# Attention and a squared-ReLU layer on one core: a third set of q and k turned by the DMA crossbar, and a new order of loads

## The chip, the core and the metric

The kernel runs on one core of one Trainium2 chip. The time is the device time of one execution in microseconds (us). The profile comes from one further execution; its span, from the first to the last instruction, is about 2 us shorter than the device time of the same run (212.7 against 214.51).

## What is computed

Four batches, eight heads, 768 positions and 64 elements a head. Each position attends to the 96 positions up to and including its own and to the first 8 positions; a bias falls linearly with the distance, by a slope of each head. The result goes through a layer of 512 to 2048 with a squared ReLU and back to 512.

```python
scores = (q @ k.T) / sqrt(64) - slope[h] * dist      # kept: local (96) or global (first 8)
a = softmax(scores)                                  # per head
x = (a @ v)                                          # heads side by side: 3072 x 512
h = maximum(x @ w_in, 0)                             # 512 x 2048
out = (h * h) @ w_out                                # 2048 x 512
```

Inputs and output are float32; the kernel works in float16 with float32 sums.

## The kernel before

The 3072 rows are cut into eight **half batches** of 384 rows, numbered 0 to 7; batch b holds the halves 2b and 2b+1, and a half is three tiles of 128 rows. While TensorE computes the two layers of one half, the attention of the next half is laid between its matmuls. Halves 0 and 1 are the opening, and are worked through tile by tile.

A list scheduler in the kernel (`Plan`) lays out all operations by estimated durations and writes them in that order, engine by engine. The PE queue and the queue of loads keep the order in which they are listed; all else is placed by its estimated readiness. So constants such as a load's duration or an operation's `lag` change the order in which instructions stand, not what they do.

All loads are cast from float32 to float16 and issued by GpSimd (POOL). Half 0 and 1 and half 2 are turned (q and k brought to the layout with the head's elements on partitions) by TensorE transposes into PSUM, with copies by ACT or DVE behind them. Halves 3 to 7 are turned by the DMA crossbar, issued by SyncE (SP), as are the stores of the output and the turning of the attention's result into the layer's input `xt`:

```python
def list_loads(x):
    prev = halves[x.hb - 2] if x.hb >= 2 else None
    before = (prev.turned if prev else []) + ([*halves[x.hb - 1].turned, prev.x_ops[NPAIR - 1]] if x.hb > 3 else [])
    ...
            if x.hb > 3 and name == "sq" and t == 0:
                for turn in halves[x.hb - 1].turns + halves[x.hb - 2].turns[-1:]:
                    behind(dma, turn)                  # this load waits for those crossbar transfers
    ...
        x.q_in = [rows(q, "sq", t) for t in range(HT)]      # three loads of 128 rows each
        x.k_in = [rows(k, "sk", t) for t in range(HT)]
        x.v_in = [rows(v, "v", t) for t in range(HT)]

def turn(x, a):                                        # half 2 alone, pair of heads a
    # six 128x128 transposes into one PSUM bank, two copies to qk
    ...
                    nc.tensor.transpose(out=trp[:, i, t, :], in_=st[:, t, 2 * a:2 * a + 2, :],
                                        identity=ident)

def turn_by_dma(x):                                    # halves 3 to 7
    for i, (name, loads) in enumerate((("sk", x.k_in), ("sq", x.q_in))):
        def emit(e, i=i, name=name):
            turn = nc.sync.dma_start_transpose(
                out=x.bt.qk[:, 1 - i, ts]..., in_=getattr(x, name)...)
            if not x.turns:
                behind(turn, x.last_load)              # the first waits for the last load of q and k
            x.turns.append(turn)
        op = plan.add({"SP": 1.7}, emit, [*loads, x.bt.op, *late])
        op.lag = 2.5
    for a in range(NPAIR):
        x.qk_ops[a] = x.turned + [plan.add(*fix_k(x, a), x.turned[:1], wait=4.0)]   # kb: small DVE copies

def to_x_by_dma(x, a):                                 # xt, one crossbar transfer for each of 4 pairs
    ...
            x.turns.append(nc.sync.dma_start_transpose(out=x.xt[:, a, :]..., in_=st["tm"]...))
```

`score` issues the q-k products (`sp`, line 464), `attend` the products with v (`av`, line 519), `layer1` the first layer (`hps`, line 560; it needs `xt` of all four pairs), `layer2` the second (`yps`, line 609; four steps of four matmuls for each tile of 128 rows). `PLACES` says after how many steps of the layers each score, turn and attend of the next half stands; `OPENING` is the order on TensorE of the first two halves (T turns a tile, S scores it, A attends, X turns the result, F, G, D, E are parts of layer 1), and `LOADING` the order of the first loads (v, k and q by tile, c the quarters of `w_in`). `warm` adds matmuls on zeros where the plan sees a gap in the opening.

```python
for name in OPENING.split():
    jobs[name]()
for job in l1(x1, 8) + l2(x0)[:6]:
    job()
for hb in range(1, NHB):
    x = halves[hb]
    for y in halves[2:4] if hb == 1 else halves[hb + 2:hb + 3]:
        list_loads(y)
    main = l2(x0)[6:] + l2(x) if hb == 1 else l1(x) + l2(x)
    side = attention(halves[hb + 1]) if hb + 1 < NHB else []
    merge(main, side)
    if hb + 2 < NHB:
        turn_by_dma(halves[hb + 2])
```

Of the kernel before, what the change touches and what calls it, by code (L numbers as in the profile page):

```python
# [16 lines left out]

OPENING = """T0 T2 S0o S1b A01 S1o A00 T3 S2b X01 S2o A10 A11 T4 S3b V1 X00 X11 A21 S4o A20 F1 X21 S3o  # L20
X10 S4b X20 F0 G00 V2 T5 V3 V4 G11 A30 G10 A31 S5o G30 G31 S5b A41 G01 F3 X30 G21 A40 X31 F2
X40 X41 G20 A50 E00 A51 E01 E11 X50 X51 E10 D0 D1"""

LOADING = """v0 k2 q2 k3 v2 v1 q3 v4 k4 q4 c1 c0 q5 k5 v3 c3 v5 c2"""

PLACES = {2: (3, 7, 7, 9, 10, 11, 1, 0, 1, 0),
          0: (0, 9, 7, 11, 16, 18), 1: (0, 9, 9, 11, 17, 19)}


class Op:
# [113 lines left out]
def kernel(  # L149
# [42 lines left out]
    def bank(shape, dtype, name, i=0):  # L192
        return ps_p.tile(shape, dtype, name=name, tag=f"ps{plan.now[i]}")
# [4 lines left out]
    def copy(e, out, in_):  # L198
        if e == "ACT":
            nc.scalar.copy(out=out, in_=in_)  # L200
        else:
            eng(e).tensor_copy(out=out, in_=in_)  # L202
# [5 lines left out]
    def warm(ps):  # L208
        fp32 = ps.dtype == FP32
        n = min(512, ps.shape[-1]) if fp32 else P  # L210
        for _ in range(int(plan.spare / (n / 2400 + 0.003))):
            if fp32:
                nc.tensor.matmul(ps[:, 0:n], lhsT=zero[:, 0:P], rhs=zero[:, 0:n], start=True,
                                 stop=True)
            else:
                nc.tensor.transpose(out=ps[:, 0:n], in_=zero[:, 0:P], identity=ident)
# [85 lines left out]
    def list_loads(x):  # L302
        r0 = x.half * HALF
        prev = halves[x.hb - 2] if x.hb >= 2 else None
        before = (prev.turned if prev else []) + ([*halves[x.hb - 1].turned, prev.x_ops[NPAIR - 1]] if x.hb > 3 else [])
        vbefore = [halves[x.hb - x.half - 3].attended[-1]] if x.hb >= 4 else []

        def rows(src, name, t, rank=None):
            def emit(e):
                dst = (x.bt.v[:, x.half * HT + t, :, 0:D] if name == "v"  # L310
                       else staged(x, name)[:, t, :, :])
                dma = nc.gpsimd.dma_start(out=dst, in_=src[x.b, :, r0 + t * P:r0 + (t + 1) * P, :]  # L312
                                          .rearrange("h p d -> p h d"))
                if x.hb > 3 and name == "sq" and t == 0:
                    for turn in halves[x.hb - 1].turns + halves[x.hb - 2].turns[-1:]:
                        behind(dma, turn)
                if name == "sk":
                    x.last_load = dma
            return plan.load(0.86, emit, vbefore if name == "v" else before, rank,
                             1.6 if x.hb == 0 else 2.6)  # L320

        if x.half == 0:
            def start(e):
                new_batch(x.bt)
                nc.vector.memset(x.bt.v[:, :, :, D:D + 1], 1.0)
            x.bt.op = plan.add({"DVE": 0.1}, start, vbefore, rank=0)
        if x.hb > 1:
            x.q_in = [rows(q, "sq", t) for t in range(HT)]
            x.k_in = [rows(k, "sk", t) for t in range(HT)]
            x.v_in = [rows(v, "v", t) for t in range(HT)]  # L330
        else:
            x.k_in, x.q_in, x.v_in = [None] * HT, [None] * HT, [None] * HT
            for t in range(HT):
                r = x.half * HT + t
                if r > 1:
                    for src, name, key, ops in ((k, "sk", "k", x.k_in), (q, "sq", "q", x.q_in)):
                        load_jobs[f"{key}{r}"] = lambda src=src, name=name, ops=ops, t=t: (
                            ops.__setitem__(t, rows(src, name, t, -3 if not plan.queues["LOAD"]
                                                    else None)))
                load_jobs[f"v{r}"] = lambda t=t: (  # L340
                    x.v_in.__setitem__(t, rows(v, "v", t)), x.v_in[t].needs.append(x.bt.op))
            return
        for l in x.v_in:
            l.needs.append(x.bt.op)
        x.bt.v_in = [*getattr(x.bt, "v_in", []), *x.v_in]
# [24 lines left out]
            out=w_in_sb[:, :, c * n:(c + 1) * n],  # L370
            in_=moe_w_in[:, c * n:(c + 1) * n].rearrange("(k p) f -> p k f", p=P)))

    def list_w_out():
        n = NFT // 4
        for c in range(4):
            w_out_op.append(plan.load(2.55, lambda e, c=c: nc.gpsimd.dma_start(
                out=w_out_sb[:, c * n:(c + 1) * n, :],
                in_=moe_w_out[c * n * P:(c + 1) * n * P, :].rearrange("(m p) d -> p m d", p=P))))

# [13 lines left out]
    def fix_k(x, a):  # L393
        t0, t1 = tiles_before(x)

        def emit(e):
            kt = x.bt.qk[:, 1, :, a, :]
            copy(e, x.bt.kb[:, a, t0 - 1:t1 - 1, GR:P], kt[:, t0:t1, GR:P])
            copy(e, x.bt.kb[:, a, t0 - 1:t1 - 1, 0:GR],
                 kt[:, 0:1, 0:GR].to_broadcast([P, t1 - t0, GR]))  # L400
        return {"DVE": 0.2 + 0.08 * (t1 - t0)}, emit

    def turn(x, a):
        state = {}

        def emit(e):
            state["ps"] = trp = bank([P, 2, HT, P], FP16, "trp")
            warm(trp.rearrange("p i t c -> p (i t c)"))
            for i, st in enumerate((x.sq, x.sk)):
                for t in range(HT):  # L410
                    nc.tensor.transpose(out=trp[:, i, t, :], in_=st[:, t, 2 * a:2 * a + 2, :],  # L411
                                        identity=ident)
        job = plan.pe(6 * 0.056, emit, x.q_in + x.k_in + [ident_op], 1)

        def evac(i):
            def emit(e):
                copy(e, x.bt.qk[:, i, x.half * HT:(x.half + 1) * HT, a, :], state["ps"][:, i])
            return plan.after(job, {"ACT": 0.39, "DVE": 0.31}, emit)
        ops = [evac(0), evac(1)]
        x.turned.append(job)  # L420
        x.qk_ops[a] = ops + [plan.add(*fix_k(x, a), [ops[1]])]


    def turn_by_dma(x):
        ts = slice(x.half * HT, (x.half + 1) * HT)
        late = list(halves[x.hb - 2].x_ops.values()) if x.hb > 3 else []
# [3 lines that stand above are left out]
                    out=x.bt.qk[:, 1 - i, ts].rearrange("p t a c -> p (t a) c"),  # L430
                    in_=getattr(x, name).rearrange("p t h d -> p (t h d)"))
                if not x.turns:
                    behind(turn, x.last_load)
                x.turns.append(turn)
            op = plan.add({"SP": 1.7}, emit, [*loads, x.bt.op, *late])
            op.lag = 2.5
            x.turned.append(op)
        for a in range(NPAIR):
            x.qk_ops[a] = x.turned + [plan.add(*fix_k(x, a), x.turned[:1], wait=4.0)]
# [356 lines left out]
    def attention(x):  # L796
        jobs = []
        places = PLACES[x.hb if x.hb == 2 else x.half]
        for k in range(len(TOGETHER[x.half])):
            jobs.append((places[k], lambda k=k: score(x, k)))  # L800
        for a in range(NPAIR):
            if x.hb == 2:
                jobs.append((places[6 + a], lambda a=a: turn(x, a)))
            jobs.append((places[2 + a], lambda a=a: attend(x, a)))
            jobs.append((places[2 + a], lambda a=a: to_x_by_dma(x, a)))
        return sorted(jobs, key=lambda j: j[0])
# [28 lines left out]
    for name in LOADING.split():  # L835
# [6 lines left out]
                           rank=0) for h in range(H)]  # L842
    mask_ops = [plan.add({"ACT": 0.43}, lambda e, h=h: fill_mask(h), [dist_op], rank=10 + h)
                for h in range(H)]
    list_w_out()

    jobs = {}
    for r in range(NT):
# [17 lines left out]
        job()  # L866
    for hb in range(1, NHB):
        x = halves[hb]
        for y in halves[2:4] if hb == 1 else halves[hb + 2:hb + 3]:
            list_loads(y)  # L870
        if hb == 1:
            fix_v(halves[2].bt, 1, 2)
        main = l2(x0)[6:] + l2(x) if hb == 1 else l1(x) + l2(x)
        if hb == NHB - 1:
            main = main[:-NFT // 4] + [lambda: last_layer2(x, HT - 1)]
# [3 lines that stand above are left out]
            t0, t1 = tiles_before(halves[hb + 2])  # L879
            for t in range(t0, t1):  # L880
                fix_v(halves[hb + 2].bt, t, t + 1)
            turn_by_dma(halves[hb + 2])
# [37 lines left out]
```

The softmax here doesn't subtract the row's maximum and nothing guards it: scores larger than these inputs give would overflow.

## Time and profile before

| | |
|---|---|
| device time, median of 3 runs | 214.99 us (214.2 to 215.36) |
| span of the profiled run | 212.7 us, granted TensorE clock 1.000 |
| TensorE busy (PE) | 206.0 us, 97% |
| VectorE (DVE), ScalarE (ACT), GpSimd (POOL) busy | 116.7, 122.0, 66.6 us |
| DMA of the loads (q0), of SP's transfers (q1) | 13.11 MB each |
| layer 2 starts on TensorE (first `yps`) | 45.04 us |
| layer 1 of half 2 starts (`hps` after the first scores of half 3) | 70.63 us |

In the profile every instruction has its engine, its line of the kernel, and its tiles as "out<-in". PEld is TensorE's loading of weights, which runs beside its matmuls. SPq and POOLq are the sequencers that issue DMAs; for such a row the duration is that of issuing, and "to landing" is the time from the start of issue until the data are there. Line numbers are those of the kernel before.

### The profile page before, as it was taken

Reading aid. Unit: us, or ns where it says so; the run is one execution under the profiler, and the core shown is the slowest. Engines: PE = TensorE matmul, PEld = TensorE weight load, DVE = VectorE, ACT = ScalarE, POOL = GpSimd, SP = SyncE. Lnnn points to the kernel's source line nnn. Section 1 sums busy time; section 2 is a strip of 40 time slices with the busy share of each in tenths; the row PEclk is TensorE's granted clock in tenths of the full one; section 3 lists DMA queues with packets and bytes.
Section 4 is the critical chain, followed back from the end, with each engine's and each line's share of the span. In section 5 each row is a group of like instructions: output and inputs, shape, how many; then the busy total and the mean of one; then the engine's idle time right before and its main releaser. Section 6 shows DMA issues by size and latency. Waiting matters only on the chain.

```text
span 212.7 us, 4804 instructions
## 1 busy us (share of the span) xinstructions
PE 206.0 (97%) x1908; PEld 127.3 (60%) x1908; DVE 116.7 (55%) x334; ACT 122.0 (57%) x250; POOL 66.6 (31%) x82
## 2 busy tenths in 40 slices
PE   6799999999999999999999999999999999999994
PEld 7587889755464565456654665456644665456553
DVE  7598987443582579409770679219860777114300
ACT  6789985644741885148821994148811994237421
POOL 8994643694000940095006800094000000000000
PEclk9999999999999999999999999999999999999999
DMA  6999999999935999599976997299952100320012
GB/s 176 166 174 188 191 207 210 161 154 163 201 120 154 107 154 154 133 118 172 148 113 119 158 135 146 73 137 177 130 121 99 52 18 19 89 99 2 0 52 99
DMA packets 106343, 27.06 MB, mean 127 GB/s; under 512 B 96976, under 2 KB 103376, under 8 KB 106320
## 3 DMA queue, kind: packets, MB, share of 16 engines
q0 software_dynamic: 74944, 13.11, 80.2%
q1 hardware_dynamic: 30320, 13.11, 26.7%
q10 hardware_dynamic: 1056, 0.52, 0.8%
q8 instruction: 15, 0.25, 0.5%
q14 instruction: 8, 0.07, 0.1%
HBM read 27.26 MB, written 6.29 MB: 158 GB/s over the span
## 4 chain that ended last, share of the span: by engine, by line
PE 93%; DMA 3%; POOL 1%; DVE 1%; ACT 0%; issue 0%; POOLq 0%
PE hps L560 40%; PE yps L609 37%; PE sp L464 4%; PE av L519 4%; DMA sq<-in_q_dram 3%; PE yps L637 2%; PE sp L721 2%; PE av L760 1%; PE sp L714 1%; PE trp L669 1%; PE trx L787 1%; PE trp L411 1%; POOL v L312 0%; POOL sk L312 0%; DVE tm L772 0%; ACT qk L200 0%
## 5 line engine op out<-in xcount | busy, mean ns | idle before, releaser
L560 PE MATMUL hps<-xt,w_in_sb 128*128 128x384 f16 (+2 forms) x608 | 88.5, 301 | 0.0
L609 PE MATMUL yps<-w_out_sb,h 128*128 128x512 f16 x368 | 83.0, 379 | 0.0
L560 PEld LDWEIGHTS <-w_in_sb 128*128 128x128 f16 x608 | 53.8, 98 | 26.6
L584 ACT ACTIVATE hr<-hps 128x384 f16<-128x384 f32 (+1 forms) x106 | 54.9, 526 | 14.4 <-PE hps L560 13.3
L609 PEld LDWEIGHTS <-h 128*128 128x128 f16 x368 | 34.9, 98 | 39.0
L200 ACT COPY y<-yps 128x512 f32<-128x512 f32 (+1 forms) x25 | 14.2, 569 | 66.4 <-PE yps L609 63.8
L595 DVE TENSOR_TENSOR h<-hr 128x768 f16<-128x768 f16 (+1 forms) x70 | 35.5, 519 | 23.2 <-ACT hr L584 22.8
L312 POOL DMA_DIRECT2D sq<-in_q_dram x22 | 19.4, 889 | 66.0 <-DMA xt<-tm 64.3
L477 ACT ACTIVATE ex<-sp 128x512 f16<-128x512 f32 x66 | 35.0, 621 | 1.2 <-PE sp L464 1.2
L586 DVE TENSOR_SCALAR hr<-hps 128x384 f16<-128x384 f32 (+1 forms) x16 | 9.0, 562 | 39.4 <-PE hps L560 39.4
L312 POOL DMA_DIRECT2D v<-in_v_dram x24 | 21.7, 926 | 4.4 <-DMA w_out_sb<-in_moe_w_out_dram 3.7
L497 DVE TENSOR_TENSOR phat<-ex,mask 128x1024 f16<-128x1024 f16 (+1 forms) x36 | 20.2, 596 | 2.4 <-ACT ex L477 2.4
L312 POOL DMA_DIRECT2D sk<-in_k_dram x22 | 19.5, 901 | 5.0 <-DMA w_out_sb<-in_moe_w_out_dram 3.1
L529 DVE TENSOR_TENSOR tm<-av,rec 128x384 f16<-128x384 f32 x24 | 13.4, 557 | 0.8
L519 PEld LDWEIGHTS <-phat 128*128 128x128 f16 x240 | 9.8, 97 | 3.1
L519 PE MATMUL av<-v,phat 128*128 128x65 f16 x144 | 10.9, 193 | 0.0
L202 DVE COPY vb<-v 128x520 f16<-128x520 f16 (+1 forms) x32 | 9.9, 309 | 1.6 <-DMA v<-in_v_dram 0.9
L519 PE MATMUL av<-vb,phat 128*128 128x65 f16 x96 | 10.1, 194 | 0.0
L202 DVE COPY kb<-qk 128x96 f16<-128x96 f16 (+4 forms) x56 | 8.1, 203 | 2.0 <-ACT qk L200 2.0
L464 PEld LDWEIGHTS <-qk 64*128 64x128 f16 x168 | 6.3, 94 | 4.6 <-issue 3.7
L464 PE MATMUL sp<-qk 64*128 64x128 f16 x168 | 8.8, 218 | 0.0
L527 DVE RECIPROCAL rec<-av 128x6 f32<-128x6 f32 x24 | 4.7, 194 | 7.0 <-PE av L519 6.6
(66 smaller groups left out, 136.6 us busy)
## 6 DMA issues: line engine op xcount, KB each, us to landing
out_dram<-y SPq DMA_DIRECT2D x23, 256.0 KB, 2.2
v<-in_v_dram POOLq DMA_DIRECT2D x24, 128.0 KB, 6.5
sk<-in_k_dram POOLq DMA_DIRECT2D x22, 128.0 KB, 6.2
sq<-in_q_dram POOLq DMA_DIRECT2D x22, 128.0 KB, 5.6
w_in_sb<-in_moe_w_in_dram POOLq DMA_DIRECT2D x4, 512.0 KB, 10.1
w_out_sb<-in_moe_w_out_dram POOLq DMA_DIRECT2D x4, 512.0 KB, 14.1
y<-in_k_dram ACTq DMA_DIRECT2D x2, 256.0 KB, 4.9
y<-in_q_dram SPq DMA_DIRECT2D x2, 256.0 KB, 4.4
```

The costliest lines, as they stand in the source:

```text
L200: nc.scalar.copy(out=out, in_=in_)
L202: eng(e).tensor_copy(out=out, in_=in_)
L312: dma = nc.gpsimd.dma_start(out=dst, in_=src[x.b, :, r0 + t * P:r0 + (t + 1) * P, :] .rearrange("h p d -> p h d"))
L464: nc.tensor.matmul(sp[h][:, i, :], lhsT=lhsT, rhs=bt.qk[rows, 0, r, a, :], start=True, stop=True)
L477: nc.scalar.activation(out=st["ex"][:, h], in_=sp[h], func=AF.Exp, scale=scale)
L497: eng(e).tensor_tensor(out=x.phat[a][:, :, t0:t0 + n], op=ALU.mult, in0=st["ex"][:, :, i0:i0 + 2 * n].rearrange("p e (t b) c -> p e t (b c ...
L519: nc.tensor.matmul(av[:, h, j, :], lhsT=lhsT, rhs=rhs, start=not before, stop=before or r == 0)
L529: nc.vector.tensor_tensor(out=st["tm"].rearrange("p t e d -> p e t d"), in0=av[:, :, :, 0:D], in1=rec[:, :, :, None].to_broadcast([P, 2, H ...
L560: nc.tensor.matmul(st["ps"][:, i * n:(i + 1) * n], lhsT=w_in_sb[:, kk, m * P:(m + 1) * P], rhs=x.xt[:, kk, c0:c1], start=kk == 0, stop=kk ...
L584: nc.scalar.activation(out=o, in_=i, func=AF.Relu)
L595: eng(e).tensor_tensor(out=x.h2[:, m0:m0 + width, c0:c1], in0=hr, in1=hr, op=ALU.mult)
L609: nc.tensor.matmul(st["ps"], lhsT=x.h2[:, m, j * P:(j + 1) * P], rhs=w_out_sb[:, m, :], start=m == 0, stop=m == NFT - 1)
```

## The change

Half 2 is now turned by the crossbar like halves 3 to 7, so that its TensorE transposes and their PSUM copies fall away (`turn` is gone). For that its q and k must be there earlier: their six loads are listed ahead of the last quarter of `w_out`. The loads of half 3 now wait until half 2's crossbar transfers have landed, as the loads of the later halves already did for their predecessors. Order of the opening and of the first loads, and the places of half 2's scores and attends and of the odd halves' attends, are new.

```diff
-OPENING = """T0 T2 S0o S1b A01 S1o A00 T3 S2b X01 S2o A10 A11 T4 S3b V1 X00 X11 A21 S4o A20 F1 X21 S3o
-X10 S4b X20 F0 G00 V2 T5 V3 V4 G11 A30 G10 A31 S5o G30 G31 S5b A41 G01 F3 X30 G21 A40 X31 F2
-X40 X41 G20 A50 E00 A51 E01 E11 X50 X51 E10 D0 D1"""
+OPENING = """T0 T2 S0o S1o S2b V1 S1b A00 T3 V2 A01 S2o A10 S3o A11 A21 T4 X11 X01 S3b A20 X00 T5 X21 S4o
+X20 X10 F1 S4b A31 G11 V3 G10 G01 F0 A41 X31 A30 G00 S5b A40 F3 X30 G30 F2 X41 V4 X40 S5o
+G21 E10 E00 E11 A50 G20 A51 X50 G31 X51 E01 D0 D1"""
-LOADING = """v0 k2 q2 k3 v2 v1 q3 v4 k4 q4 c1 c0 q5 k5 v3 c3 v5 c2"""
+LOADING = """v1 q2 k2 k3 q3 v0 v2 q5 q4 k4 k5 c1 v3 c0 v4 c3 c2 v5"""
-PLACES = {2: (3, 7, 7, 9, 10, 11, 1, 0, 1, 0),
-          0: (0, 9, 7, 11, 16, 18), 1: (0, 9, 9, 11, 17, 19)}
+PLACES = {2: (5, 7, 8, 10, 11, 12),
+          0: (0, 9, 7, 11, 16, 18), 1: (0, 9, 9, 12, 17, 18)}
...
-        before = (prev.turned if prev else []) + ([*halves[x.hb - 1].turned, prev.x_ops[NPAIR - 1]] if x.hb > 3 else [])
+        before = (prev.turned if prev else []) + (halves[x.hb - 1].turned if x.hb > 2 else [])
+        before = before + ([prev.x_ops[NPAIR - 1]] if x.hb > 3 else [])
...
-                if x.hb > 3 and name == "sq" and t == 0:
+                if x.hb > 2 and name == "sq" and t == 0:
...
+            if x.hb == 2:
+                list_w_out(0, 3)
             x.q_in = [rows(q, "sq", t) for t in range(HT)]
             x.k_in = [rows(k, "sk", t) for t in range(HT)]
+            if x.hb == 2:
+                list_w_out(3, 4)
             x.v_in = [rows(v, "v", t) for t in range(HT)]
...
-            w_out_op.append(plan.load(2.55, ...
+            w_out_op.append(plan.load(2.55 if c < 3 else 3.6, ...
...
-    def turn(x, a):                       # the whole function falls away
...
-            op.lag = 2.5
+            op.lag = 2.5 if x.hb > 2 else 5.5
...
-            if x.hb == 2:
-                jobs.append((places[6 + a], lambda a=a: turn(x, a)))
...
-    list_w_out()
+    list_loads(halves[2])
+    turn_by_dma(halves[2])
...
-        for y in halves[2:4] if hb == 1 else halves[hb + 2:hb + 3]:
+        for y in halves[3:4] if hb == 1 else halves[hb + 2:hb + 3]:
```

In the built programs TensorE has 30 matmuls fewer: the 24 transposes of half 2, and six of the matmuls on zeros in the opening. SP issues two crossbar transfers more, ahead of all stores of the output; half 3's two crossbar transfers stand ahead of half 2's four `xt` transfers on SP, as before.

More of the change, by code (lines that the diff above doesn't have):

```diff
@@ L371, in load_w_in, with list_w_out @@
             in_=moe_w_in[:, c * n:(c + 1) * n].rearrange("(k p) f -> p k f", p=P)))
-    def list_w_out():
+    def list_w_out(c0, c1):
         n = NFT // 4
-        for c in range(4):
-            w_out_op.append(plan.load(2.55, lambda e, c=c: nc.gpsimd.dma_start(
+        for c in range(c0, c1):
+            w_out_op.append(plan.load(2.55 if c < 3 else 3.6, lambda e, c=c: nc.gpsimd.dma_start(
                 out=w_out_sb[:, c * n:(c + 1) * n, :],
@@ L401, in fix_k @@
         return {"DVE": 0.2 + 0.08 * (t1 - t0)}, emit
-    def turn(x, a):
[L404 to L421, printed above, removed]
     def turn_by_dma(x):
```

## The prediction

> **What bounds the kernel now.** I read the busy shares first, then the waits of TensorE alone, then its chain in order of time around half 2, then SP's own timeline, because the change moves work from TensorE to SP and the DMA engines.
>
> ```profile
> PE 206.0 (97%) x1908; PEld 127.3 (60%) x1908; DVE 116.7 (55%) x334; ACT 122.0 (57%) x250; POOL 66.6 (31%) x82
> ```
>
> TensorE is busy 97% of the span; no other engine passes 57%. The waits of PE from 9.5 us to the end are these two rows (us in total, times, longest):
>
> ```profile
> PE trp L669 <- DMA sq<-in_q_dram: 1.0, 1, 1.0
> PE sp L721 <- ACT qk L200: 0.4, 1, 0.4
> ```
>
> The first ends at 9.49 us. After it TensorE waits 0.4 us once, at 18.4 us. So what is taken off TensorE comes off the time, unless a new wait arises. The chain of work, in order of time (start, us, what), around half 2:
>
> ```profile
> 45.04 5.18 PE yps L609 x24
> 50.22 0.67 PE trp L411 x12
> ...
> 51.75 0.67 PE trp L411 x12
> ...
> 69.86 0.78 PE sp L464 x24
> ```
>
> These show the removed work (L411: 12 transposes in 0.67 us, twice) and the stage's end: layer 1 of half 2 starts at 70.63. SP in the same stage:
>
> ```profile
> 53.35 1.54 SPq L429 DMA_TRANSPOSE qk<-sq  x1
> 54.99 2.16 SPq L429 DMA_TRANSPOSE qk<-sk  x1
> 57.20 1.40 SPq L624 DMA_DIRECT2D out_dram<-y  x2
> 60.34 1.19 SPq L541 DMA_TRANSPOSE xt<-tm  x1
> 62.99 0.33 SPq L624 DMA_DIRECT2D out_dram<-y  x1
> 63.42 3.85 SPq L541 DMA_TRANSPOSE xt<-tm  x3
> ```
>
> The first two rows turn half 3. SP issues in order, so half 2's four xt transfers stand behind them. The last xt lands at 68.38 by the trace, 2.25 us before 70.63 needs it. That reserve, not the 57% of any engine, is what the change may use up.
>
> **What the Trainium skill says.** "VectorE: DVE Perf Modes", section "The three transpose paths", gives one 128x128 turn 390 ns on TensorE and 1309 ns by crossbar. The trace has 56 ns each in a row of 12 on TensorE (0.67/12), and 4.4 us from issue to landing for the 12 blocks of half 3's q. Both see the crossbar as the slower path; it pays only where its time is hidden. "DMA: Bandwidth & Descriptors", section "Issuing engines are not separate DMA queues", says that transfers from all issuers interleave on the same 16 DMA engines. The trace agrees: a 256 KB store issued by SP at 49.14, while POOL's loads filled the engines, needed 5.9 us to land, against a median of 2.2:
>
> ```profile
> out_dram<-y SPq DMA_DIRECT2D x1, 256.0 KB, 5.9
> out_dram<-y SPq DMA_DIRECT2D x23, 256.0 KB, 2.2
> ```
>
> (the first from the DMA issues of 42 to 56 us, the second from the page). No page bears on the order of the opening.
>
> **The change part by part.**
>
> 1. *Transposes removed.* 2 x 0.67 = 1.34 us off TensorE, all on the path. Their eight PSUM copies (five on ACT at 488 ns, three on DVE) lay beside it and bring nothing.
>
> 2. *The opening.* From 9.49 to 45.04 TensorE has 35.55 us. In it lie 0.44 us of idle time and seven matmuls on zeros: three of 0.056 us (0.17) and four that take 0.46 (11.70 to 12.16). The most that an order can bring is so 1.07 us. The new order keeps one such matmul. By the order of the two built programs it puts 22 more real matmuls ahead of F1 (about 22 x 0.056 = 1.22 us), so F1 would start at 9.49 + (9.68 - 1.07) + 1.22 + 0.11 = 19.43. Its quarter c1 of w_in is now the 12th load: the tenth landed at 15.87, one more is about 0.95 and a quarter 2.45, so 19.3: in time. c0 comes at 19.3 + 1.0 + 2.5 = 22.8, while G01 would be reached near 22.6: a wait of 0.2. What is left after F1 is 25.87 - 1.22 = 24.65 us, so layer 2 starts at 19.43 + 0.2 + 24.65, about 44.3 instead of 45.04. ACT is full from 10 to 22 us and may add some tenths. I take 0.75 us for it.
>
> 3. *Half 2's q and k.* The load stream has no gap: the third quarter of w_out landed at 36.90 and the fourth 2.55 later; q and k of half 2 took from 39.45 to 45.01, that is 5.56. With the order changed, k ends at 36.90 + 5.56 = 42.5, and the fourth quarter at 45.0. Layer 2 needs it 12 matmuls in, at 44.3 + 12 x 0.216 = 46.9: reserve 1.9 us, of which the transfers now running beside it may take one. Half 2's scores stand 44 yps after the start: 44.3 + 9.5 = 53.8.
>
> 4. *How long half 2's turning takes.* It is issued at 42.6, when the fourth quarter and the three loads of v (landing about 48 to 49) still fill the engines. The store above moved 256 KB in some 5 us beside loads: about 50 KB per us. Half 3's two turns (393 KB each) ended 2.67 us after the last load landed (59.05 - 56.38): near 255 KB per us. So by 48.5 about 250 of 786 KB are through, and the rest takes 2.1 us: landed at 50.5. Scores at 53.8 are safe.
>
> 5. *Half 3 then starts late.* Its loads wait for this landing. In the later cycles the last load of k lands 9.8, 10.5, 11.2 and 10.4 us after the first of q is issued (68.99 to 78.77, and so on); here the first is issued at 50.5 instead of 41.90, and I take 10.3: 60.8. SP then issues the two turns in 1.54 + 2.16 and a little, 3.9: 64.7. Only then come four xt of 1.3 each and a store of 0.45: 70.35, and 1.1 until the last lands (67.26 to 68.38): about 71.4.
>
> 6. *When it is needed.* From the start of layer 2 to that of layer 1 of half 2 are 25.59 us, less 1.34: 24.25. So TensorE would be there at 44.3 + 24.25 = 68.55, and meets the missing fourth xt after three matmuls, 0.5 us later. Wait: 71.4 - 69.05 = 2.35 us.
>
> Sum: -1.34 - 0.75 + 2.35 = +0.26 us. Behind this stage nothing changes: the later halves' turning has 7 us to spare (half 4's k landed at 86.37, scored at 93.84), and TensorE has the same matmuls.
>
> **The rivals.**
>
> *A: nothing waits.* Then -2.1 us, 212.9. For it: TensorE has no other gap, and the reserve of 2.25 us in the stage is of the same size as the delay; if half 2's turning lands at 48, the moment v does, the chain ends at 68.9 and TensorE never sees it. Against it: the 5.9 us of the store beside loads.
>
> *B: the wait of step 6*, 215.2, or up to 216.5 if the turning lands at 51.5. SP's queue becomes the bound for one stage. For it: the order on SP is fixed, half 3's turns ahead of half 2's xt, and their loads start 8.6 us later than before (50.5 against 41.90), while the stage needs its xt 2.1 us earlier.
>
> *C: the fourth quarter of w_out is late*, a wait in the second four-step of yps near 47 us of up to 1 us. Against it: in the trace loads hardly slowed beside SP's transfers (pitch 0.9 to 1.2 us against 0.9). If B holds, C costs nothing more, since B's chain hangs on the DMA, not on TensorE.
>
> *D: the opening gets worse* through ACT, 0.5 us. With B it is likewise hidden.
>
> **Range and chances.** A and B are 2.3 us apart, and which of them holds turns on one landing time that I know to about 1.2 us. My sum says 215.2; each microsecond that the turning lands earlier gives one back until -2.1 is reached, and the error of the sum is therefore lopsided to the fast side. I weigh A with 0.4 and B with 0.6: 0.4 x 212.9 + 0.6 x 215.3 = 214.3, rounded to 214.4 for the opening's risk. Range 212.6 to 216.4: A with a little more luck in the opening, B with a landing at 51.5. 2% are 4.3 us; neither is near it.
>
> **What would show it.** No row for L411's transposes, and PE busy less by about 2. The first yps near 44.3 (step 2). Half 2's last k landed near 42.5 and its turns near 50.5 (3, 4). The first load of half 3 issued then, its turns on SP from about 60.8, the last xt near 71.4 (5). A new wait of PE hps for DMA xt of about 2.3 us, and the first hps of half 2 near 71 (6); under A no such row, and that hps near 68.6. Wrong altogether I would be if the waits of PE show w_out, kb or ACT for more than 1 us, or if a later stage, unlike before, has a gap.

## The result and the profile after

The changed kernel takes **219.94 us** (median, 218.65 to 220.47) against 214.40 in the same comparison: ratio 1.024, 95% interval 1.0202 to 1.0278. It is slower by 5.5 us; 214.4 (212.6 to 216.4) was predicted. The profiled execution took 220.47 us and is the slowest of the six; its span is 218.7 us, those of the six are 216.9 to 218.7. Lines are those of the changed kernel from here: `hps` is line 544, `yps` 593, `sp` 448, crossbar turns 413, `xt` 525. The views of the experiments have line numbers of their own; go by the tiles there.

The engines' busy row of the page of the changed kernel (busy us, share of the span, instructions):

```profile
PE 208.1 (95%) x1878; PEld 127.1 (58%) x1878; DVE 115.4 (53%) x329; ACT 120.4 (55%) x247; POOL 66.6 (30%) x82
```

And TensorE's waits from 52 us to the end, from the table of waits of the same run (what waited, for what; sum in us, how many, the longest):

```profile
PE hps L544 <- DMA xt<-tm: 3.3, 3, 1.5
PE sp L448 <- DMA qk<-sk: 1.0, 1, 1.0
PE sp L448 <- DVE kb L201: 0.2, 1, 0.2
```

TensorE has 30 matmuls fewer and is busy 2.1 us *longer*. The waits make 4.5 us and all lie in one place, from 67.7 to 74.2 us: 1.2 us at half 3's first scores and 3.3 us among the first matmuls of half 2's layer 1. TensorE had reached those scores at 67.72, 2.14 us earlier than before (69.86): the 0.80 of the opening and the 1.34 of the transposes had both been gained up to there. SP's timeline shows where the waits come from:

```profile
42.09 1.87 SPq L413 DMA_TRANSPOSE qk<-sq  x1
44.07 4.20 SPq L413 DMA_TRANSPOSE qk<-sk  x1
48.34 8.23 SPq L608 DMA_DIRECT2D out_dram<-y  x3
62.54 1.49 SPq L413 DMA_TRANSPOSE qk<-sq  x1
64.14 3.13 SPq L413 DMA_TRANSPOSE qk<-sk  x1
67.38 1.20 SPq L525 DMA_TRANSPOSE xt<-tm  x1
68.67 0.53 SPq L608 DMA_DIRECT2D out_dram<-y  x1
69.30 3.79 SPq L525 DMA_TRANSPOSE xt<-tm  x3
```

Half 2 is turned from 42.09 on, half 3 from 62.54 (53.35 before), and the first xt is issued at 67.38 (60.34 before). By the trace the turning of half 2 lands at 51.85, the last xt at 74.20. The chain of work now runs through exactly these transfers (start, us, what):

```profile
44.07 7.78 DMA qk<-sk
...
64.14 4.52 DMA qk<-sk
...
71.88 2.32 DMA xt<-tm
74.20 0.04 issue
74.24 7.96 PE hps L544 x33
```

Its last row holds what I had not thought of. In the chain of the kernel before, 36 of these hps took 5.96 us:

```profile
70.63 5.96 PE hps L560 x36
```

Here 33 take 7.96. The table of stretches (us, PE busy, ..., and after POOL's column the granted clock) tells why:

```profile
70.00:72.00 2.00, 0.47 (x2) 0.10 (x1) 0.00 (x0) 2.00 (x5) 0.00 (x0) 1.00 0.52 147
72.00:74.00 2.00, 0.48 (x1) 0.10 (x1) 0.00 (x0) 0.02 (x1) 0.00 (x0) 0.60 0.35 77
74.00:76.00 2.00, 1.76 (x6) 0.84 (x6) 1.25 (x3) 0.00 (x0) 1.25 (x2) 0.50 0.68 262
76.00:78.00 2.00, 2.00 (x7) 0.88 (x6) 1.27 (x4) 0.98 (x2) 2.00 (x3) 0.50 1.23 78
78.00:80.00 2.00, 2.00 (x10) 1.05 (x9) 1.50 (x3) 0.85 (x2) 2.00 (x4) 0.69 1.90 124
```

TensorE is nearly idle from 70.15 to 74.24: two hps alone lie in between. Within this stretch, at 72.4, its clock is halved (the mean of 0.60 from 72 to 74 us gives the moment), and it comes back at 79.2 (the mean of 0.69 from 78 to 80). The 5.0 us from 74.24 to 79.2 at half the clock lose half of that, 2.5 us. "Busy" hides this: a slow matmul counts as busy. From 82 us on the matmuls of a stage take as long as before.

### The profile page after: what moved, and what is told of

It is laid out like the page before. It is cut to its first block, busy times and chain, and to the rows that moved or that the text cites. A ratio compares the mean times of both kernels' runs of the same rounds, so it can differ in the third digit from the quotient of the medians.

```text
span 218.7 us, 4745 instructions
## 1 busy us (share of the span) xinstructions
PE 208.1 (95%) x1878; PEld 127.1 (58%) x1878; DVE 115.4 (53%) x329; ACT 120.4 (55%) x247; POOL 66.6 (30%) x82
## 4 chain that ended last, share of the span: by engine, by line
PE 64%; DMA 20%; POOL 9%; SPq 2%; issue 1%; DVE 1%; ACT 0%; POOLq 0%
PE hps L544 30%; PE yps L593 27%; DMA sk<-in_k_dram 7%; DMA w_out_sb<-in_moe_w_out_dram 6%; DMA qk<-sk 6%; PE av L503 3%; PE sp L448 3%; POOL sq L312 3%; POOL v L312 2%; POOL sk L312 2%; PE yps L621 2%; SPq L413 2%; POOL w_in_sb L373 1%; DMA xt<-tm 1%; SPq L525 1%
## 5 line engine op out<-in xcount | busy, mean ns | idle before, releaser
L544 PE MATMUL hps<-xt,w_in_sb 128*128 128x384 f16 (+2 forms) x608 | 90.9, 306 | 3.3 <-DMA xt<-tm 3.3
L544 PEld LDWEIGHTS <-w_in_sb 128*128 128x128 f16 x608 | 54.8, 99 | 32.1 <-issue 6.7
L199 ACT COPY y<-yps 128x512 f32<-128x512 f32 (+1 forms) x24 | 13.6, 567 | 68.4 <-PE yps L593 65.9
L570 DVE TENSOR_SCALAR hr<-hps 128x384 f16<-128x384 f32 x15 | 8.3, 554 | 39.1 <-PE hps L544 39.1
L201 DVE COPY kb<-qk 128x96 f16<-128x96 f16 (+4 forms) x56 | 7.4, 201 | 8.0 <-DMA qk<-sk 7.8
L448 PE MATMUL sp<-qk,kb 64*128 64x128 f16 x96 | 7.3, 216 | 0.2 <-DVE kb L201 0.2
```

Of the source, the lines that this page charges most:

```text
L448: nc.tensor.matmul(sp[h][:, i, :], lhsT=lhsT, rhs=bt.qk[rows, 0, r, a, :], start=True, stop=True)
L544: nc.tensor.matmul(st["ps"][:, i * n:(i + 1) * n], lhsT=w_in_sb[:, kk, m * P:(m + 1) * P], rhs=x.xt[:, kk, c0:c1], start=kk == 0, stop=kk ...
```

## The experiments

**Theory.** Half 2's turning lands late; half 3's loads wait for it; half 3's two turns stand ahead of half 2's xt on SP and carry the delay to TensorE, which waits and then loses its clock. **Rivals:** the new opening costs; the clock falls for a reason of its own; loads and crossbar transfers crowd each other on the DMA engines whatever SP's order; the late loads alone hold TensorE up.

### The new order alone (r1_new_order_alone)

The kernel before with the new `OPENING` and `LOADING`, and `1: (0, 9, 9, 12, 17, 18)` in `PLACES`.

> The kernel before with only the new opening, the new order of the first loads and the new places of the odd halves; half 2 is turned by TensorE as before. Theory (the opening brings 0.8 us, and the loss is made wholly by the chain of half 2's crossbar turning): about 213.6 us, the first yps near 44.2, no wait on xt. Rival (the new order itself costs something later, which the changed kernel hides behind its wait): 214.4 or more, with a gap on TensorE after 45 us.

Measured: 213.77 us against 214.43, ratio 0.9968 (0.9956 to 0.9980). First yps at 44.22, no wait over 0.3 us after 9.5 us. The new order is a gain of 0.66 us; it is not the cause.

### The gap filled (r2_gap_filled)

```diff
                 warm(st["ps"])
+                if x.hb == 2 and ms[0] == 0:
+                    for _ in range(18):
+                        nc.tensor.matmul(st["ps"], lhsT=zero[:, 0:P], rhs=zero, start=True, stop=True)
```

> The changed kernel with 18 matmuls on zeros (3.9 us) put ahead of half 2's first layer-1 matmul, where TensorE would wait for xt. Theory (TensorE's clock fell to 0.5 from about 72.5 to 79 us because it had stood idle; that costs about 2.6 us beside the wait): clock 1.0 throughout, about 217.3 us, the 36 hps of that stretch at 0.163 us each again. Rival (the clock falls for another reason, or the slow matmuls wait for data): unchanged at 219.5 to 220, or longer by what the added matmuls take.

Measured: 218.43 us, ratio 1.0187 (1.0173 to 1.0202). Adding 3.9 us of matmuls makes the kernel 1.5 us faster by the medians and 2.0 us by the spans of the two profiled executions (216.7 against 218.7). The two intervals of the ratio touch at 1.0202; the views of the run are clearer. From its chain of work:

```profile
70.34 3.99 PE hps L544 x18
74.34 5.85 PE hps L547 x36
```

And one row of its table of stretches:

```profile
72.00:74.00 2.00, 2.00 (x11) 0.92 (x10) 0.00 (x0) 0.49 (x1) 0.00 (x0) 1.00 0.28 61
```

The clock stays at 1.00 and the 36 real hps take 5.85 us again. So idling had cost the clock, 1.5 to 2 us of the 5.5. I had put 217.3. The last xt lands as late as in the changed kernel (74.09), and the three hps that had slipped in between the waits now come after the fill, 0.5 us; the rest of the 1.1 us is open.

### The old opening under the change (r8_old_opening)

The changed kernel with the two old strings `OPENING` and `LOADING`.

> The changed kernel with the opening and the order of the first loads of the kernel before. Theory (the end of the stage hangs on the DMA and SP chain, which begins with the load stream, not on TensorE): layer 2 starts near 45 instead of 44.1, but the turning, the xt transfers and the start of layer 1 of half 2 are where they are in the changed kernel, so 219 to 220 us: the better opening is lost in the wait. Rival (TensorE's own sequence sets the time): 0.8 us slower than the changed kernel, 220.7.

Measured: 218.93 us, ratio 1.0213 (1.0200 to 1.0226), 0.1 us below what was expected: not slower than the changed kernel, though layer 2 starts 0.6 us later (44.72). Half 2's turning lands at 51.81, its last xt at 73.54, 0.7 us earlier than in the changed kernel. The DMA and SP chain sets the time, and the better opening is lost in the wait.

### Half 3 turned by TensorE (r11_half3_by_tensore)

```diff
...                                       (the function `turn` of the kernel before is there again)
+        if hb == 1:
+            side = sorted(side + [(14 + a, lambda a=a: turn(halves[3], a)) for a in range(NPAIR)], ...)
         merge(main, side)
...
-            turn_by_dma(halves[hb + 2])
+            if hb != 1:
+                turn_by_dma(halves[hb + 2])
```

> The changed kernel, but half 3, not half 2, is turned by TensorE: 24 transposes and eight PSUM copies at steps 14 to 17 of the stage. Half 2's crossbar turning, its late landing near 51.9 and the wait of half 3's loads for it all stay; only half 3's two crossbar transfers ahead of xt on SP fall away. Theory (the delay reaches TensorE through these two transfers on SP): no wait on xt or on half 3's q and k, clock 1.0, 1.34 us of transposes back on TensorE: 213.6 to 214.2 us, that is the time of the new order alone. Rival (the late loads of half 3, landing near 62.5, or xt beside loads hold TensorE up whatever SP issues first): waits of 1 us or more stay, 215.5 or more.

Measured: **213.80 us**, ratio 0.9965 (0.9953 to 0.9977), as expected and the same as the new order alone. Half 2's turning lands at 51.87 and half 3's k at 62.32, both as late as in the changed kernel. But SP's timeline of this run has no half-3 turns, and xt is issued at 60 us:

```profile
60.00 1.20 SPq L546 DMA_TRANSPOSE xt<-tm  x1
61.29 0.53 SPq L629 DMA_DIRECT2D out_dram<-y  x1
61.91 3.85 SPq L546 DMA_TRANSPOSE xt<-tm  x3
```

Its table of TensorE's waits from 9.5 us to the end has two rows, both short:

```profile
PE sp L726 <- DVE qk L201: 0.4, 1, 0.4
PE trx L792 <- DVE tm L777: 0.3, 1, 0.3
```

This settles the place of the cause. Half 2's late turning and the late loads that follow from it do not hold TensorE up by themselves; half 3's two crossbar transfers, made late by them and standing ahead of xt on SP, do. This run takes away both their place in SP's order and their traffic; the next one changes the order alone.

### xt first (r3_xt_first) and scores later (r4_xt_first_scores_later)

```diff
-        late = list(halves[x.hb - 2].x_ops.values()) if x.hb > 3 else []
+        late = list(halves[x.hb - 2 if x.hb > 3 else 2].x_ops.values()) if x.hb > 2 else []
```

and for the second also `3: (8, 11, 12, 14, 17, 18)` in `PLACES`, for half 3.

> The changed kernel with half 3's two turns made to wait for half 2's four xt transfers, so that SP issues xt first; nothing else. Theory (SP's fixed order carries the delay): xt lands near 66 and no longer holds up layer 1; instead half 3's scores, which still stand ahead of it at 67.7, wait for half 3's turns, which end near 71.5. PE waits 3.5 to 4 us there, 217 to 220 us. Rival (the xt transfers are slow in themselves, whatever stands ahead): xt still lands after 70 us.

> As the one before, and half 3's scores stand 8 and 11 steps into layer 1 of half 2 instead of 0 and 9, its attends at 12, 14, 17, 18. Theory: with xt first and the scores near 73 us neither waits, so both gains of the change come through, 214.4 - 0.8 - 1.34 = 212.3 us; up to 213 if half 4's later turning pushes half 3's xt a little. Rival (contention of the DMA engines, not the order, sets the end): still above 215.

Measured: 221.38 us (ratio 1.0330, 1.0299 to 1.0361) and 216.36 us (1.0087, 1.0053 to 1.0121), both slower than expected. In the first the last xt lands at 68.98 instead of 74.20, so SP's order does carry the delay, though 66 had been expected. The wait moves from xt to half 3's scores, and is longer than the 3.5 to 4 us expected. From the first one's table of waits:

```profile
PE sp L448 <- DMA qk<-sq: 6.2, 1, 6.2
```

And from its timeline of SP:

```profile
65.83 1.39 SPq L608 DMA_DIRECT2D out_dram<-y  x1
67.39 1.64 SPq L413 DMA_TRANSPOSE qk<-sk  x1
69.12 0.87 SPq L608 DMA_DIRECT2D out_dram<-y  x1
70.15 1.48 SPq L413 DMA_TRANSPOSE qk<-sq  x1
```

SP issues these four without a gap of more than 0.2 us: half 3's two turns stand behind a store each, and the second lands only at 73.85. With later scores (r4) most of the loss goes, but not all: the first xt was issued at 60.15 and landed only at 66.70, while half 3's loads of v ran until 66.49 (in r12 below, which moves these loads away, the first xt was issued at 59.88 and landed at 62.63). Waits of 1.2, 0.6 and 0.2 us stay, 2.0 of the 4 us above what was expected; the rest is open.

### Half 3's loads free (r5_half3_loads_free)

```diff
-        before = ... + (halves[x.hb - 1].turned if x.hb > 2 else [])
+        before = ... + (halves[x.hb - 1].turned if x.hb > 3 else [])
-                if x.hb > 2 and name == "sq" and t == 0:
+                if x.hb > 3 and name == "sq" and t == 0:
```

> The changed kernel, but half 3's loads do not wait for half 2's turning, as it was in the kernel before. Theory (what runs beside the turning sets its length, and the wait of the loads passes this on): half 3's loads follow v at once, its k is there near 53.5, but half 2's turning, beside loads until about 57, lands at 55 to 57 instead of 51.9, so half 2's scores wait some 2 to 4 us at 53.7; half 3's turns then follow within 5 us, xt ahead of 70. Total 214 to 217 us. Rival (the turning is slow in itself and loads beside it do not matter): it lands at 52 as before, nothing waits, 212.3 us.

Measured: 218.63 us, ratio 1.0192 (1.0172 to 1.0212). Half 2's turning lands at 57.01 and its scores wait 3.2 us, as expected, but the time is above the 214 to 217 expected. I had left out the clock again: eight yps behind the wait take 3.53 us where they took 1.73. Nor was xt early: its last transfer lands at 74.19. The wait that the change gives half 3's loads is so not its mistake; without it another wait arises, and 1.3 us at most are won.

### Fewer loads beside the turnings (r6, r7, r9, r10, r12)

r6 lists half 2's v behind half 3's q and k; r7 also loads half 2's q and k after two quarters of `w_out`; r10 loads them ahead of all of `w_out`; r9 is r10 with half 3's v behind half 4's q and k; r12 is the changed kernel with that v and with xt first. Attends and scores are moved as the expectations say. "The same" in the expectation of r10 means r9, whose expectation stands below it; half 3's attends are not moved in r10.

> The changed kernel with half 2's three loads of v moved behind half 3's q and k, and half 2's attends at steps 11 to 14 instead of 8 to 12. Beside half 2's turning then stands only the last quarter of w_out. Theory: the turning lands near 48 instead of 51.9, half 3's turns are issued near 58.7, the last xt lands near 70 instead of 74.2, TensorE waits about 1 us instead of 4.5, its clock stays up: 213 to 214 us. Rival (the turning takes its 8 to 10 us whatever runs beside it): it still lands after 51, and the time is 219 or more, since the attends stand later too.

> As the one before, and half 2's q and k loaded between the second and third quarter of w_out, so that they land near 39.5 instead of 42.1. Theory: turning issued at 39.6 beside two quarters, landed near 46.5 to 47; half 3's turns near 57.5, the last xt near 68.8; no wait on TensorE: both gains come through, 212.3 to 213 us. Rival: beside twice as much w_out the turning takes until 49 or later, and nothing is won against the one before.

> The same with half 3's v where it was, so that its three loads run beside half 3's turning until about 64. Theory: half 2's turning lands near 48.3 as in the one before, but half 3's k lands only near 65.5 to 66 and xt near 71 to 72; TensorE waits 2 to 3 us, with a slower clock behind: 216 to 218 us. If loads beside the turning do not matter: the same time as the one before.

> The changed kernel with half 2's q and k loaded ahead of all of w_out (turning issued near 35.3, with all of w_out and v to run beside), and with half 3's v loaded behind half 4's q and k, so that no load runs beside half 3's turning and half 2's xt; half 3's attends at steps 17 to 20. Theory (loads beside a crossbar transfer set its length, at about 50 KB/us while they run, 255 KB/us after): half 2's turning lands near 48.3, half 3's is issued near 58.8 and takes 5 us, the last xt lands near 68.5: no wait, or a few tenths, on TensorE; 212.3 to 213 us, below the kernel before and below the new order alone (213.8). Rival (the chain on SP is too long whatever is loaded when): the last xt after 71, 217 us or more.

> The changed kernel with half 2's xt ahead of half 3's turns on SP, those two turns directly one behind the other, half 3's v loaded behind half 4's q and k, half 3's scores at steps 7 and 10, its attends at 17 to 20. Theory: with no load beside them the xt transfers are issued from 60 to 65.5 and landed by 67; half 3's turns are issued at 65.6 and landed near 71.5, needed at 72.3; half 4 follows 2 us later than before, which its reserve takes: no wait over 0.5 us, 212.4 to 213.5 us, faster than the new order alone. Rival (some further transfer or DVE's bunched work takes the place): 214.5 or more.

Measured: 218.99, 219.14, 220.16, 221.23 and 221.15 us (in the order of the expectations), ratios 1.019 to 1.033, all intervals clear of 1. As repairs all five failed. They measure the turning, though (from the issue of the first to the landing of the second transfer; times from the trace):

| turning | issued, landed | takes, us | loads beside it until |
|---|---|---|---|
| half 3, r12 (k first) | 67.06, 72.64 | 5.6 | none |
| half 3, r9 | 61.93, 67.90 | 6.0 | none |
| half 2, r6 | 42.29, 48.41 | 6.1 | 45.22 |
| half 3, changed kernel | 62.54, 68.66 | 6.1 | 66.11 |
| half 3, r10 | 61.95, 68.29 | 6.3 | 65.75 |
| half 2, changed kernel | 42.09, 51.85 | 9.8 | 47.70 |
| half 3, r6 | 59.46, 70.00 | 10.5 | 66.15 |
| half 2, r5 | 42.09, 57.01 | 14.9 | 61.94 |
| half 2, r9 | 34.64, 52.47 | 17.8 | 52.40 |

Alone it takes 5.6 to 6 us; some 3 to 4 us of loads beside it add little, 5.6 and 6.7 us of them add 4 us; and under a queue of loads that runs on it takes 15 to 18 us. In r9 and r10 it ends with that queue, in r5 5 us before it. There it slows the loads too: in r9 and r10 the last three quarters of `w_out` land 3.0 to 3.4 us after the one before, instead of 2.5. In r6 half 2's turning was 3.4 us earlier as expected, but v's six loads then ran beside half 3's. In r9 and r10 starting 7 us earlier brought nothing, and 0.4 us of difference between their turnings of half 3 shows that its three loads of v are not what makes it long. r9's last xt (73.95) and time came out as its rival said, because half 2's turning landed at 52.47 instead of 48.3; that the chain is too long whatever is loaded when is not shown. In r12 the turns were in time (0.5 us of wait), but the late v made the attends wait 4.3 us.

No version got both gains. The one to keep is the new order with TensorE's turning, r1, or r11, both 0.3% below the kernel before.

## Why the prediction was wrong

The mechanism was the one on record as rival B and steps 4 to 6. Steps 4 and 5 put the last xt at 71.4, it landed at 74.20; and step 6 priced the wait at its length alone, while the halved clock behind it cost 2.5 us more.

- **Step 1, transposes:** right. r11 puts them back in four groups of 0.34 us, 1.34 in all.
- **Step 2, opening:** right. First yps at 44.08 instead of 44.88 in the timeline, 0.80 us; 0.75 was said.
- **Step 3, loads:** right. Half 2's k landed at 42.08 (42.5 said), the last quarter of `w_out` at 44.65 (45.0).
- **Step 4, the turning:** mis-sized. 51.85 instead of 50.5. The rates of 50 and 255 KB/us came from one store and one turning; the table above shows that no such pair of rates holds. At 255 KB/us a turning with nothing beside it would take 3.1 us (786 / 255); r9's took 6.0. (By its own 50 KB/us, step 4 should have had 238 KB/us instead of 255, and 295 KB through by 48.5 instead of 250; the landing at 50.5 stays.)
- **Step 5, half 3:** the loads took 10.7 us (62.54 - 51.85) for 10.3 said; the two issues on SP 4.84 (67.38 - 62.54) for 3.9, because the second took 3.13 us instead of 2.16; the rest 6.82 (74.20 - 67.38) for 6.7. With step 4 the last xt is 2.8 us later than said.
- **Step 6, the wait:** 4.5 us for 2.35, including 1.2 us at half 3's scores, which the prediction did not consider.
- **What was missing:** the clock. 33 hps at the former pace would take 33 x 5.96 / 36 = 5.46 us; they took 7.96, 2.5 us more, and r2 shows by its removal that the idling brings it. "TensorE: Matmul & The Clock Gate", section "What's actually happening", of the Trainium skill says that the array drops to half its clock after an idle window of about 3.4 us. The trace agrees in kind only: the clock fell at 72.4, when TensorE had been nearly idle for 2.2 us, with one hps of 0.32 us in them; in r5 it fell 2.4 us after the last matmul.

Sum: -1.34 - 0.80 + 4.45 + 2.5 = 4.8 us; the span grew by 6.0. Of the remaining 1.2 us, 0.65 are the three hps between the waits (0.34, 0.32 and 0.48 us in place of 0.163 each), and 0.3 lie after the last copy.

Rival A, weighed with 0.4, did not occur: it needed a landing at 48, and even in r6, with only the last quarter of `w_out` beside it, the turning landed at 48.41. C and D did not occur: no wait on `w_out`, and a better opening.

## What to carry to other kernels

When a sequencer issues in order, price a new transfer by what stands behind it: here two transfers of the *next* half, made late, stood ahead of the ones that the current half needed, and taking them off SP gave the whole 5.5 us back and more. A wait on TensorE can cost more than its length, and so can several short ones close together: here 4.5 us of waits brought 2.5 us of slow matmuls. Add these to the estimate, and if the wait can't be removed, fill it. Work moved from a full engine to "free" DMA time needs that time to be free in that stage: here the crossbar path took 6 us alone and 10 beside loads, to save 1.34.

## What the runs showed of the hardware

- One wait of 3.2 us halved TensorE's clock (r5), and so did three waits of 0.7, 1.0 and 1.0 us between 70.2 and 73.6 us, with single matmuls between them (r8). Waits of 0.6 and 1.2 us, with 5.5 us of matmuls between them (r4), did not. Matmuls on zeros in the gap kept it at 1.00 (r2).
- Once fallen, the clock stayed at 0.50 for 6.8 us (changed kernel, r3, r5, r9, r10) or 3.4 us (r6, r8, r12), by the traces.
- It need not fall in every execution of a kernel: of r6's four, two had a mean clock of 0.998 and 0.999 and took 217.29 and 217.58 us, two had 0.992 and 0.984 and took 220.52 and 220.40.
- The second of two crossbar turns one behind the other holds SP 1.6 to 7.0 us for its issue alone. The longest are those under a full queue of loads (7.0 in r9 and r10), but loads do not explain the whole: with none beside it, it was 3.04 us in r9 and 1.68 in r12. SP's timeline of r9, half 2 under a full queue, then half 3 with no load beside it:

```profile
34.64 4.42 SPq L423 DMA_TRANSPOSE qk<-sq  x1
39.16 6.99 SPq L423 DMA_TRANSPOSE qk<-sk  x1
...
61.93 1.29 SPq L423 DMA_TRANSPOSE qk<-sq  x1
63.33 3.04 SPq L423 DMA_TRANSPOSE qk<-sk  x1
```

Why the second takes 3 us in r9 with no load beside it stays open.
